# Early rows gathered once, from candidates of both column halves: an attention and expert-routing kernel with a speculative first group

## The chip, the core and the metric

The kernel runs on one core of one Trainium2 chip. The metric is device time in microseconds, the median of three runs. The engines are TensorE (PE; its weight loads are listed as PEld), VectorE (DVE), ScalarE (ACT), GpSimd (POOL) and SyncE (SP), which here does nothing but issue transfers. The 16 DMA engines serve SyncE's queue and GpSimd's gathers and scatters. TensorE's clock has two levels, 2.4 and 1.2 GHz; the profile shows which was granted as 1.00 and 0.50.

## What is computed

Block-local attention, then a mixture of experts with a capacity:

```python
# q, k, v: (8, 8, 576, 64); blocks of 64 positions
scores = scale * q_c @ k_c.T          # inside each block
attn = softmax(scores); out = attn @ v_c
x = out.transpose(0, 2, 1, 3).reshape(4608, 512)

logits = x @ w_gate                   # 8 experts
expert_idx = argmax(logits); gate_w = its softmax probability
for e in range(8):
    tok = tokens with expert_idx == e
    if len(tok) > capacity: keep the `capacity` (80) with the largest gate_w
    out[tok] = gate_w * (relu(x[tok] @ w1[e]) @ w2[e])   # w1: 512x1024, w2: 1024x512
# tokens that are not kept have zero rows
```

## The kernel before

**Attention, 0 to about 113 us.** 18 pairs of half tiles run through one pipeline written out by hand (`scores`, `maxima`, `minus`, `probs`, `values`, `divide`, `store`). The rows go to a scratch array `xs` in memory, and at the same time through a transposition (`xtrans`) and the gate product (`gate_mm`, `gate_copy`, `gate_sum`), four tiles of 128 tokens at a time. `values(35)`, `xtrans(17)`, `gate_mm(8)` are the last of these.

**Which tokens are kept.** A token's gate probability is turned into one of 256 levels. For each tile, `signs` (on ScalarE) or `steps_` (on VectorE) compare all levels with each token's, and `tally` sums these over the tokens of an expert by short matmuls; `left_add` adds them up in `left`. `threshold` counts the levels that at least `capacity` tokens reach. Tokens at or over the threshold become candidates: they are numbered by prefix sums, one-hot matrices (`hot`) move their row numbers and keys into a table (the matmuls of line 1034, into `two`), and exact ranks select 80 of them (lines 1042 to 1131). `place` then writes the row numbers of the expert slots, GpSimd gathers those rows, and `experts` runs the two layers in groups of 128 slots.

**The speculative first group.** From the first 28 tiles alone the kernel guesses a stricter threshold for experts 0 and 1 (`spec_count` to `spec_slot`) and numbers 64 early rows of each in `ptc`. `spec_hot` makes one-hots of that number on VectorE, in three groups of 10, 9 and 9 tiles (`SHOT`). `spec_cand` multiplies them with the tokens' row numbers (`comp`), and `spec_gather` sums three pieces into an index `gi0` and has GpSimd gather the rows into `x0`. `spec_units` cuts the first group's two expert layers into 19 units of work: 3 of transpositions and 16 of matmuls, each four column groups wide. `fill(k)` puts the next k units into TensorE's order, between the short steps of the selection. Each engine works strictly in program order. So where `fill(1)` puts the first unit, the transposition of `x0`, TensorE waits until the gather has landed.

`keep_warm(n)` puts n matmuls of 256 columns whose result nobody reads into TensorE's order.

**Transfers.** SyncE issues in program order: the last stores to `xs` and pieces of the weights of experts 0 and 1 (`early_pieces`), then the 2 MB loads of the other experts' weights (line 1155) with nine zeroings of the output (`clear`, 1 MB each) between them. Those loads go into buffers laid over memory of the attention stage, so each waits for the last use of what lay there; the first of them lies over `pk0`, which holds the early one-hots. The six scatters of result rows (line 266) wait until all zeroings have landed.

Of the kernel before, what the change touches and what calls it, by code (L numbers as in the profile page):

```python
# [8 lines left out]
F32 = mybir.dt.float32  # L9
BF16 = mybir.dt.bfloat16  # L10
# [7 lines left out]
P = 128  # L18
# [23 lines left out]
S0 = 64  # L42
# [16 lines left out]
def attention_moe(ctx: ExitStack, tc: tile.TileContext, qk, vv, wg, w1, w2, cap, cst, out):  # L59
# [116 lines left out]
    def rows(t, at, n=NT * 512):  # L176

        return nc.gpsimd.indirect_dma_start(
            out=t, out_offset=None, in_=xs[0:n, :],
            in_offset=bass.IndirectOffsetOnAxis(ap=at, axis=0),  # L180
            bounds_check=n - 1, oob_is_err=False)
# [117 lines left out]
    with ExitStack() as actx:  # L299
# [432 lines left out]

        def spec_hot(r0, n):
            if 'hot0' not in S:
                S['hot0'] = wk.tile([P, 3, S0, 10], BF16, name="pk0", tag="qb1", bufs=1), deque(range(3))
            oh = S['hot0'][0][:, S['hot0'][1].popleft()]
            nc.vector.tensor_tensor(
                oh[:, :, 0:n], S['io_h'][:, 0:S0, 0:n],
                S['ptc'][:, None, r0:r0 + n].to_broadcast([P, S0, n]), op=ALU.is_equal)
            S['oh0', r0] = oh  # L740

        def spec_cand(r0, n):
            oh = S['oh0', r0]
            if 'cand0' not in S:
                S['cand0'] = ps1.tile([P, 2, 512], F32, name="xw0", tag="tp")[:, 0]
            cand0 = S['cand0'][0:S0, 0:12].rearrange("p (k e) -> p k e", e=2)
            k = 2 * S.setdefault('chunk0', 0)
            S['chunk0'] += 1
            for j in range(n):
                rt = r0 + j  # L750
                nc.tensor.matmul(
                    cand0[:, k:k + 2, :],
                    lhsT=oh[:, :, j], rhs=comp[:, rt, 0:2, 0:2], start=j == 0, stop=j == n - 1)

        def spec_gather():
            gi0 = mp.tile([P, 2], I32, name="gi0")
            with nc.allow_low_precision(reason="row numbers are whole and far below 2^24"):
                nc.vector.tensor_reduce(
                    gi0[0:S0], S['cand0'][0:S0, 0:12].rearrange("p (k e) -> p e k", e=2),
                    axis=AX.X, op=ALU.add)  # L760
            x0 = S['x0'] = mp.tile([P, DM], F32, name="x0")
            for e in range(2):
                rows(x0[S0 * e:S0 * e + S0], gi0[0:S0, e:e + 1], 6 * 576)

        units = deque()

# [68 lines left out]
        with tc.manual_schedule():  # L835
# [117 lines left out]
            spec_pos()  # L953
            values(35, "s")
            spec_slot()
            for r0, n in SHOT:
                spec_hot(r0, n)
            xtrans(16)
            gate_mm(7)
            gate_copy(7)  # L960
            for j in range(24, 28):
                signs(j)
            for r0, n in SHOT:
                spec_cand(r0, n)
            divide(34)
            spec_gather()
            divide(35)
            store(17)
            early_pieces(20)
            gate_sum(7, gates)  # L970
            pops(2)
            spec_own()
            xtrans(17, ("o", "s"))
            gate_mm(8)
            flush(gates)
            gate_copy(8)
# [4 lines left out]
            two = ps1.tile([P, 2, 512], F32, name="two", tag="s")  # L981
            S['warm'] = [ps1.tile([P, 512], F32, name=("xw", "hw", "pwarm")[j], tag=f"o{j}") for j in range(3)]
            spec_units()
            signs(28)
            signs(29)
            gate_sum(8, gates)
            tally(24, 4)
            fill(1)
            pops(2)
            signs(30)  # L990
            signs(31)
            left_add(24)
            flush(gates)
            rest(32, "sum")
            signs(32)
            for j in range(33, 36):
                steps_(nc.vector, j)
            fill(1)
            tally(28, 4)
            left_add(28)  # L1000
            spec_keep()
            fill(1)
            tally(32, 4)
            fill(1)
            threshold()
            rest(32, "inverse", "key")
            fill(1)
            mask = gk.tile([P, NE, RT], BF16, name="mask", tag="mask", bufs=1)
# [313 lines left out]
```

## Time and profile before

| | |
|---|---|
| median of 3 runs | 240.28 us (239.45 to 240.59) |
| the profiled execution | 242.49 us, span of its trace 240.6 us |
| TensorE busy | 220.5 us, 92% of the span |
| VectorE, ScalarE, GpSimd busy | 118.5, 69.4, 54.3 us |
| moved by DMA | 84.73 MB, 352 GB/s over the span |
| mean granted TensorE clock | 0.958 |

The busy times are sums over stages with different limits, and a matmul at half clock counts as busy for longer. What the change is worth is to be read from the stage between the end of attention and the first expert row, about 112 to 154 us, and from what the end of the kernel waits for.

### The profile page before, as it was taken

To read this page: it belongs to the slowest core of one execution; us is meant where nothing else is said; L and a number is where in the kernel's file an instruction comes from. 1 tells how busy PE (TensorE), PEld (TensorE's weight loads), DVE (VectorE), ACT (ScalarE), POOL (GpSimd) and SP (SyncE) were. 2 spreads that over 40 slices of the span, in tenths; PEclk is the share of its full clock that TensorE was granted. 3 is DMA by queue.
4 is the path that set the end of the run, shared out by engine and by line. 5 is a ranking of instruction groups with operands and counts; after the bars stand their busy time and mean duration, and the time that the engine had idled before them with its cause. 6 is when DMAs were issued, how large, how long until landed. Compare 5 with 4: busy or idle time off the path is not lost.

```text
span 240.6 us, 7297 instructions
## 1 busy us (share of the span) xinstructions
PE 220.5 (92%) x3161; PEld 139.0 (58%) x3161; DVE 118.5 (49%) x270; ACT 69.4 (29%) x123; POOL 54.3 (23%) x155
## 2 busy tenths in 40 slices
PE   8789998999999999999866989899999999999960
PEld 5689887888888898987743253234334333333310
DVE  7857686777877778788432457401111112111110
ACT  2214333453645455455423151111002011010000
POOL 9300402022322222236230351420000000000631
PEclk9999999999999999999855799999999999999997
DMA  6999999999999999999999969999999999998221
GB/s 254 403 408 378 333 396 408 410 409 405 402 395 393 379 407 332 356 352 408 395 293 399 396 240 308 412 332 362 369 406 408 403 388 399 397 408 312 99 94 40
DMA packets 34758, 84.73 MB, mean 352 GB/s; under 512 B 3038, under 2 KB 3166, under 8 KB 34720
## 3 DMA queue, kind: packets, MB, share of 16 engines
q1 hardware_dynamic: 33744, 81.31, 90.0%
q0 software_dynamic: 976, 2.88, 3.3%
q8 instruction: 27, 0.44, 0.7%
q14 instruction: 11, 0.09, 0.1%
HBM read 64.00 MB, written 20.45 MB: 351 GB/s over the span
## 4 chain that ended last, share of the span: by engine, by line
PE 78%; DMA 10%; issue 3%; ACT 2%; SPq 2%; DVE 2%; POOL 1%; POOLq 0%
PE hc L214 13%; PE o L437 12%; PE s L380 12%; PE yc L247 11%; PE px L409 4%; PE pt L409 4%; DMA qb<-in_qk 4%; DMA w<-in_w 3%; DMA x<-xs,gi 3%; PE hw L794 3%; PE yfirst L247 3%; PE small L489 3%; PE hw L785 2%; PE hpc L232 2%; PE hfirst L214 2%
## 5 line engine op out<-in xcount | busy, mean ns | idle before, releaser
L437 PE MATMUL o<-vb,pT 128*64 128x130 f32 x576 | 36.1, 276 | 0.6 <-ACT pT L418 0.5
L380 PE MATMUL s<-qb 128*64 128x128 f32 x512 | 31.9, 276 | 2.7 <-DMA qb<-in_qk 1.8
L437 PEld LDWEIGHTS o<-vb,pT 128*64 128x64 f32 x576 | 31.6, 135 | 1.8 <-ACT pT L418 0.6
L214 PE MATMUL hc<-w,xtc 128*32 128x512 f32 x288 | 32.5, 594 | 0.0
L380 PEld LDWEIGHTS s<-qb 128*64 128x64 f32 x512 | 27.9, 137 | 5.1 <-issue 3.7
L391 DVE TENSOR_REDUCE mx<-s 128x16 f32<-128x1024 f32 x18 | 22.0, 1225 | 14.7 <-PE s L380 13.9
L247 PE MATMUL yc<-w,htc 128*32 128x512 f32 x256 | 28.2, 592 | 0.0
L418 ACT ACTIVATE pT<-pt 128x1024 f32<-128x1024 f32 x18 | 18.3, 1025 | 30.8 <-PE pt L409 29.2
L480 ACT COPY xT<-px 128x1024 f32<-128x1024 f32 x17 | 17.1, 1008 | 25.5 <-PE px L409 25.5
L452 DVE TENSOR_TENSOR x<-o,rc 128x1024 f32<-128x1024 f32 (+1 forms) x20 | 22.4, 1118 | 0.7
L396 DVE TENSOR_TENSOR sm<-s,mx 128x1024 f32<-128x1024 f32 x18 | 22.1, 1228 | 0.6
L214 PEld LDWEIGHTS hc<-w,xtc 128*32 128x32 f32 x288 | 8.8, 110 | 19.4 <-issue 19.4
L247 PEld LDWEIGHTS yc<-w,htc 128*32 128x32 f32 x256 | 8.2, 110 | 18.7 <-issue 18.7
L266 POOL DMA_INDIRECT out<-x,to x1 | 1.0, 1048 | 65.4 <-DVE htc L236 65.4
L219 ACT ACTIVATE hsc<-hc 128x512 f32<-128x512 f32 x4 | 2.4, 598 | 46.4 <-PE hc L214 46.4
L590 ACT ACTIVATE lv<-io_b,bo 128x256 bf16<-128x256 bf16 x33 | 14.2, 498 | 0.3 <-DVE bo L570 0.3
L221 DVE TENSOR_SCALAR hsc<-hc 128x512 f32<-128x512 f32 x5 | 3.5, 690 | 21.8 <-PE hc L214 21.8
L252 DVE TENSOR_SCALAR ysc<-yc,gatec 128x512 f32<-128x512 f32 x4 | 3.0, 751 | 21.2 <-PE yc L247 21.2
L409 PE MATMUL pt<-ct,sm 64*128 64x64 f32 x288 | 12.8, 229 | 0.0
L409 PE MATMUL px<-ct,x 64*128 64x64 f32 x272 | 12.4, 229 | 0.2 <-issue 0.2
L236 DVE COPY htc<-hpc 128x512 f32<-128x512 f32 x5 | 3.5, 692 | 18.3 <-PE hpc L232 18.3
L409 PEld LDWEIGHTS pt<-ct,sm 64*128 64x128 f32 x288 | 10.3, 139 | 2.9 <-issue 2.8
(211 smaller groups left out, 260.8 us busy)
## 6 DMA issues: line engine op xcount, KB each, us to landing
w<-in_w SPq DMA_DIRECT2D x12, 2048.0 KB, 15.0
qb<-in_qk SPq DMA_DIRECT2D x32, 512.0 KB, 8.1
vb<-in_vv SPq DMA_DIRECT2D x36, 260.0 KB, 7.1
out<-zero SPq DMA_DIRECT2D x9, 1024.0 KB, 16.0
xs<-x SPq DMA_DIRECT2D x16, 512.0 KB, 7.6
w<-in_w SPq DMA_DIRECT2D x16, 512.0 KB, 8.1
w<-in_qk SPq DMA_DIRECT2D x4, 512.0 KB, 4.9
xs<-x SPq DMA_DIRECT2D x4, 256.0 KB, 6.1
```

The lines of the kernel that those rows point to most:

```text
L214: nc.tensor.matmul(h[o:o + 32, :], lhsT=xT[r][:, b, o:o + 32], rhs=getw(groups[r][g])[0][:, b, 512 * f:512 * f + 512], start=(b == 0), sto ...
L247: nc.tensor.matmul(y[o:o + 32, :], lhsT=hT[r][c // 4][:, c % 4, o:o + 32], rhs=getw(groups[r][g])[1][:, c, :], start=(c == 0), stop=(c == ...
L380: nc.tensor.matmul(ps[64 * u:64 * u + 64, t, P * pr:P * pr + P].rearrange("p (h k) -> p h k", h=2), lhsT=t8[:, 1, pr, u, :], rhs=t8[:, 0:3 ...
L391: nc.vector.tensor_reduce(d['mx'], d['s8'], axis=AX.X, op=ALU.max)
L396: nc.vector.tensor_tensor(d['sm'].rearrange("p c k h -> p h c k"), d['s8'], d['mx'][:, :, :, None].to_broadcast([P, 2, 8, 64]), op=ALU.sub ...
L409: nc.tensor.transpose(at[:, 64 * c:64 * c + 64], src(c)[rows], ident[rows, rows])
L418: nc.scalar.activation(d['pT'], pt, AF.Exp, scale=0.125)
L437: nc.tensor.matmul(po[64 * u:64 * u + 64, o:o + 130].rearrange("p (h x) -> p h x", h=2), lhsT=d['pT'][:, u, c:c + 64], rhs=v[:, :, pr, u, ...
L452: nc.vector.tensor_tensor(TT[T][:, r:r + nt, :].rearrange("p r (k h e) -> p (r k) h e", k=4, h=2), pov[..., 0:64], rc[:, :, :, None].to_br ...
L480: nc.scalar.copy(XT[n].rearrange("p c u j -> p u c j"), pm.rearrange("p u (c j) -> p u c j", j=64))
L489: nc.tensor.matmul(pl[32 * j:32 * j + 32].rearrange("p (u j) -> p u j", u=2), lhsT=wgp[:, pr], rhs=XT[2 * T + j // 2][:, 4 * (j % 2) + pr] ...
L590: nc.scalar.activation(lv, io_b, AF.Sign, bias=bo[:, rt:rt + 1], scale=-1.0)
```

## The change

It alters the speculative group and the order around it in these ways:

- The candidate matmuls write a table of 128 rows, expert 0 into the lower 64 and expert 1 into the upper 64 (`tile_position` picks the half of the array's columns); each tile takes two matmuls with 2 columns in place of one with 4. Behind each group stands one filler matmul.
- One gather of 128 rows takes the place of two of 64.
- The third group's nine one-hots are made on GpSimd (`spec_hot1`).
- A copy of one column into a spare part of `pk0` follows the gather on GpSimd. The first large weight load lies over `pk0`, so it now waits for this copy.
- Two groups of candidates stand ahead of the last transposition and one behind it; the index sum stands behind it too.
- Up to the threshold one unit is left, after the sums of tiles 28 to 31, and 15 fillers stand where there were 2. `threshold` stands ahead of the next unit, and the levels of tile 32 are made on VectorE.

```diff
         def spec_hot(r0, n):
             if 'hot0' not in S:
-                S['hot0'] = wk.tile([P, 3, S0, 10], BF16, name="pk0", tag="qb1", bufs=1), deque(range(3))
+                S['hot0'] = wk.tile([P, 4, S0, 10], BF16, name="pk0", tag="qb1", bufs=1), deque(range(3))
...
+        def spec_hot1(r0, n):
+            oh = S['oh0', r0] = S['hot0'][0][:, S['hot0'][1].popleft()]
+            pf = gk.tile([P, SPEC], F32, name="ptf", tag="ptf", bufs=1)
+            nc.gpsimd.tensor_copy(pf[:, r0:r0 + n], S['ptc'][:, r0:r0 + n])
+            for j in range(n):
+                nc.gpsimd.tensor_scalar(oh[:, :, j], ct[:, C_IO + P:C_IO + P + S0],
+                                        pf[:, r0 + j:r0 + j + 1], None, op0=ALU.is_equal)
+
         def spec_cand(r0, n):
...
-                nc.tensor.matmul(
-                    cand0[:, k:k + 2, :],
-                    lhsT=oh[:, :, j], rhs=comp[:, rt, 0:2, 0:2], start=j == 0, stop=j == n - 1)
+                for e in range(2):
+                    nc.tensor.matmul(
+                        cand0[S0 * e:S0 * e + S0, k:k + 2], lhsT=oh[:, :, j], rhs=comp[:, rt, 0:2, e],
+                        start=j == 0, stop=j == n - 1, tile_position=(0, S0 * e))
+                if j == n - 1:
+                    nc.tensor.matmul(S['cand0'][:, 1, 0:2 * P], lhsT=ones_b, rhs=io_b,
+                                     start=True, stop=True)
 
         def spec_gather():
...
-            for e in range(2):
-                rows(x0[S0 * e:S0 * e + S0], gi0[0:S0, e:e + 1], 6 * 576)
+            rows(x0, gi0, 6 * 576)
+            nc.gpsimd.tensor_copy(S['hot0'][0][:, 3, 0, 0:1], S['ptc'][:, 0:1])
...
             spec_slot()
-            for r0, n in SHOT:
-                spec_hot(r0, n)
+            spec_hot(*SHOT[0])
+            spec_hot(*SHOT[1])
+            spec_hot1(*SHOT[2])
             xtrans(16)
...
-            for r0, n in SHOT:
-                spec_cand(r0, n)
             divide(34)
-            spec_gather()
+            spec_cand(*SHOT[0])
             divide(35)
+            spec_cand(*SHOT[1])
             store(17)
...
             xtrans(17, ("o", "s"))
+            spec_cand(*SHOT[2])
+            spec_gather()
             gate_mm(8)
...
-            signs(28)
-            signs(29)
             gate_sum(8, gates)
             tally(24, 4)
-            fill(1)
+            keep_warm(5)
             pops(2)
-            signs(30)
-            signs(31)
+            for j in range(28, 32):
+                signs(j)
             left_add(24)
...
-            signs(32)
-            for j in range(33, 36):
+            for j in range(32, 36):
                 steps_(nc.vector, j)
-            fill(1)
+            keep_warm(5)
             tally(28, 4)
             left_add(28)
             spec_keep()
             fill(1)
+            keep_warm(3)
             tally(32, 4)
+            threshold()
             fill(1)
-            threshold()
```

What this does to VectorE's order, from the early one-hots (`pk`) to the next tiles' gate sums; `x` with `rc` is the division of tiles 34 and 35, `gi` the index sum. Before:

```order
L737 TENSOR_TENSOR pk_2222<-io_h,ptc 128x64x9 x2
L450 TENSOR_SCALAR rc_2300<-o_2175 128x8
L451 RECIPROCAL rc_2300<-rc_2300 128x8
L452 TENSOR_TENSOR x_2131<-o_2175,rc_2300 128x512
L758 TENSOR_REDUCE gi_2304<-xw_2271 64x2
L450 TENSOR_SCALAR rc_2313<-o_2209 128x8
L451 RECIPROCAL rc_2313<-rc_2313 128x8
L452 TENSOR_TENSOR x_2131<-o_2209,rc_2313 128x512
L559 TENSOR_REDUCE gm_2324<-small 128x4
```

And with the change:

```order
L452 TENSOR_TENSOR x_2131<-o_2175,rc_2281 128x512
L450 TENSOR_SCALAR rc_2307<-o_2209 128x8
L451 RECIPROCAL rc_2307<-rc_2307 128x8
L452 TENSOR_TENSOR x_2131<-o_2209,rc_2307 128x512
L559 TENSOR_REDUCE gm_2337<-small 128x4
L526 TENSOR_TENSOR sh_2333<-small,gm_2337 128x32
L724 TENSOR_REDUCE cnt<-mine 128x8
L476 COPY xT_2367<-px17s 128x512
L770 TENSOR_REDUCE gi_2389<-xw_2285 128x1
```

The index sum stood between the two divisions and now stands behind both and behind the copy of the last transposition.

GpSimd at the same place, from its last work for the keys to the levels of tiles 28 to 31 (`u`, `lb`). Before:

```order
L552 CAST comp<-r_1995 128x4x8
L178 DMA x_2306<-xs,gi_2304 64x512 x2
L564 TENSOR_SCALAR u_2327<-sx_2326 128x4
L567 TENSOR_SCALAR lb_2328<-u_2327 128x4
L556 TENSOR_SCALAR bb_2330<-lb_2328 128x4
```

And with the change:

```order
L552 CAST comp<-r_1995 128x4x8
L745 CAST ptf<-ptc 128x9
L747 TENSOR_SCALAR pk_2222<-ct,ptf 128x64 x9
L178 DMA x_2391<-xs,gi_2389 128x512
L773 COPY pk_2222<-ptc 128x1
L564 TENSOR_SCALAR u_2340<-sx_2339 128x4
```

A cast, nine one-hots and the one-column copy are new there, and one gather is gone.

TensorE, from the sums of tiles 24 to 27 (the last of them uses `lv_2269`, with the change `lv_2279`) to the count for the threshold (line 630); lines 778 and 785 are units (788 and 795 with the change), 663 fillers, and `lv_2431` (`lv_2470`) belongs to tile 31. Before:

```order
L612 MATMUL small_2389<-mine,lv_2269 128x8
L778 MATMUL xw<-ct,x_2306 128x128 x4
L785 MATMUL hw<-w_0_103,xT_2394 32x512 x2
L785 MATMUL hw<-w_1_1957,xT_2394 32x512 x2
...
L663 MATMUL pwarm<-io_b,ones_b 128x256
...
L612 MATMUL small_2389<-mine,lv_2431 128x8
L785 MATMUL hw<-w_0_103,xT_2394 32x512 x2
...
L630 MATMUL small_2389<-ge,ones_b 128x8
```

And with the change:

```order
L612 MATMUL small_2428<-mine,lv_2279 128x8
...
L663 MATMUL pwarm<-io_b,ones_b 128x256
...
L607 MATMUL small_2428<-mine,ones_b 128x8
...
L612 MATMUL small_2428<-mine,lv_2470 128x8
L788 MATMUL xw<-ct,x_2391 128x128 x4
...
L612 MATMUL small_2428<-mine,lv_2488 128x8
...
L630 MATMUL small_2428<-ge,ones_b 128x8
L795 MATMUL hw<-w_0_103,xT_2433 32x512 x2
```

The transposition of `x0`, for which TensorE waits, moved behind the sums of tiles 28 to 31, and three units of four matmuls moved behind the count.

## Rows read from the trace of the kernel before

**Rows 1.** Chain of waits, 112 to 160 us: start, length, what
```profile
118.13 0.16 DVE gi L758
120.12 7.29 DMA x<-xs,gi
127.55 1.10 PE xw L778 x4
134.06 0.12 PE small L607
134.42 1.42 PE hw L785 x8
136.01 0.17 DVE thr L633
154.40 0.86 PE xpc L203 x4
```

**Rows 2.** Windows: busy times by engine; granted clock, DMA share, GB/s stand last
```profile
114.80:118.00 3.20, 3.20 (x28) 3.20 (x28) 0.06 (x1) 1.74 (x5) 0.00 (x0) 1.00 1.04 402
118.20:135.20 17.00, 12.10 (x112) 6.44 (x115) 6.29 (x30) 3.90 (x10) 3.81 (x9) 0.50 1.02 356
```

**Rows 3.** Timeline of VectorE, 124 to 131 us
```profile
124.42 0.19 DVE L559 TENSOR_REDUCE gm<-small 128x4 f32<-128x32 f32 x1 [2.65 <-PE small L612]
129.42 0.19 DVE L563 TENSOR_REDUCE sx<-ex 128x4 f32<-128x32 f32 x1 [4.14 <-ACT ex L527]
130.46 0.68 DVE L595 TENSOR_SCALAR lv<-io_b,bo 128x256 bf16<-128x256 bf16 x3
```

**Rows 4.** Timeline of TensorE: candidates, and a unit's matmuls at either clock
```profile
114.79 3.30 PE L751 MATMUL xw<-comp,pk 128*64 128x4 bf16 x28 [0.18 <-ACT xT L480]
132.12 1.94 PE L785 MATMUL hw<-w,xT 128*32 128x512 f32 x8
145.54 1.06 PE L785 MATMUL pwarm<-w,xT 128*32 128x512 f32 x8
```

**Rows 5.** Timeline of GpSimd, its last stretch: the stores of the tokens
```profile
223.69 1.05 POOL L266 DMA_INDIRECT out<-x,to  x1 [65.39 <-DVE htc L236]
229.59 0.98 POOL L266 DMA_INDIRECT out<-ysc,to  x1 [0.28 <-issue]
234.22 0.98 POOL L266 DMA_INDIRECT out<-ysc,to  x1 [3.45 <-DVE ysc L252]
```

**Rows 6.** Windows, 140 to 220 us: clock, DMA share and GB/s stand last
```profile
140.00:160.00 20.00, 18.18 (x197) 7.68 (x195) 9.11 (x51) 4.07 (x11) 7.33 (x10) 1.00 0.88 305
160.00:220.00 60.00, 60.00 (x550) 20.72 (x552) 8.47 (x12) 7.20 (x13) 0.00 (x0) 1.00 1.04 395
```

**Rows 7.** Timeline of TensorE: rows from which prices are taken
```profile
107.17 2.00 PE L437 MATMUL o<-vb,pT 128*64 128x130 f32 x32 [0.45 <-ACT pT L418]
112.88 0.71 PE L409 MATMUL px<-ct,x 64*128 64x64 f32 x16
10.08 0.72 PE L857 MATMUL small<-warm 128*128 128x256 bf16 x5
```

**Rows 8.** Timeline of GpSimd: rows from which prices are taken
```profile
118.59 1.22 POOL L178 DMA_INDIRECT x<-xs,gi  x1 [5.55 <-DVE rc L451]
140.86 1.21 POOL L656 TENSOR_SCALAR pk<-ct,ptok 128x128 bf16<-128x128 f32 x2
148.04 1.12 POOL L178 DMA_INDIRECT xgc<-xs,gic  x1 [5.98 <-DVE bt L1056]
```

**Rows 9.** Timeline of SyncE's issues: the first large weight loads
```profile
120.33 8.57 SPq L1155 DMA_DIRECT2D w<-in_w  x3
```

**Rows 10.** Line L178, the row gathers: issue to landing
```profile
DMA to landing us min/median/max: 8.2/8.9/8.9
```

**Rows 11.** DMA queues from 122 to 123 us
```profile
q1 hardware_dynamic: 116, 0.21, 81.8%
q0 software_dynamic: 25, 0.06, 16.4%
```

More of the change, by code (lines that the diff above doesn't have):

```diff
@@ L744, in spec_cand @@
             if 'cand0' not in S:
-                S['cand0'] = ps1.tile([P, 2, 512], F32, name="xw0", tag="tp")[:, 0]
-            cand0 = S['cand0'][0:S0, 0:12].rearrange("p (k e) -> p k e", e=2)
+                S['cand0'] = ps1.tile([P, 2, 512], F32, name="xw0", tag="tp")
+            cand0 = S['cand0'][:, 0]
             k = 2 * S.setdefault('chunk0', 0)
@@ L750, in spec_cand @@
                 rt = r0 + j
-                nc.tensor.matmul(
-                    cand0[:, k:k + 2, :],
-                    lhsT=oh[:, :, j], rhs=comp[:, rt, 0:2, 0:2], start=j == 0, stop=j == n - 1)
+                for e in range(2):
[5 more added lines that the diff above has]
+                                     start=True, stop=True)
         def spec_gather():
-            gi0 = mp.tile([P, 2], I32, name="gi0")
+            gi0 = mp.tile([P, 1], I32, name="gi0")
             with nc.allow_low_precision(reason="row numbers are whole and far below 2^24"):
-                nc.vector.tensor_reduce(
-                    gi0[0:S0], S['cand0'][0:S0, 0:12].rearrange("p (k e) -> p e k", e=2),
-                    axis=AX.X, op=ALU.add)
+                nc.vector.tensor_reduce(gi0, S['cand0'][:, 0, 0:6], axis=AX.X, op=ALU.add)
             x0 = S['x0'] = mp.tile([P, DM], F32, name="x0")
-            for e in range(2):
-                rows(x0[S0 * e:S0 * e + S0], gi0[0:S0, e:e + 1], 6 * 576)
+            rows(x0, gi0, 6 * 576)
+            nc.gpsimd.tensor_copy(S['hot0'][0][:, 3, 0, 0:1], S['ptc'][:, 0:1])
         units = deque()
```

## The prediction

> **What bounds the kernel now.** I read the chain of waits first, then the engines' timelines at the places it names, then the clock, then the end.
>
> The chain has one long piece that is no engine's work: the second gather of the early rows is issued at 120.12 and lands 7.29 us later, and TensorE's four transpositions of those rows (line 778) start at 127.55 [rows 1]. TensorE is in order, so all that stands behind them waits too: the sums over the last tiles, the threshold at 136.01, and through that everything up to the first transposition of an expert row at 154.40. From there TensorE works to the end without a gap worth naming.
>
> The clock is the second thing to see. Over the 28 candidate matmuls (114.8 to 118.0) it is granted in full, right after them it falls to half, and it stays there for 17.0 us [rows 2]. Ahead of the fall TensorE did nothing but matmuls of 4 columns; the four early units behind the gather then ran at half clock.
>
> Third, a side chain: VectorE starts the last tile's gate sums at 124.42, but its next exponential sits on ScalarE behind the copy of those same transposed rows, so the sum comes at 129.42 and the levels' steps only at 130.46 [rows 3]. So the gather holds two chains at once.
>
> At the far end the six stores of tokens are not free to move. The first starts at 223.69, when the zeroing of the output has landed; they follow each other (the fifth at 229.59, so 1.475 us each); only the sixth, at 234.22, waits for TensorE's last product [rows 5]. The DMA engines are full from 160 to 220 us (share 1.04) and have room only before: 0.88 over 140 to 160, that is 2.4 us [rows 6]. A gain of TensorE beyond some 3 us therefore meets this second chain.
>
> **The change, part by part.**
>
> *Candidates.* 28 matmuls become 56, each for one half of the output columns. The old ones go at 3.30/28 = 118 ns [rows 4]. The trace has no pair of 64-wide halves with two columns; the nearest is line 437, which alternates between the same two column halves with far longer rows and takes 2.00 us for 32, 60 ns each [rows 7]. I take 60 (118 is the other bound): 38 ahead of the last transposition, 2.3 us, and 18 behind it, 1.1. Each of the three groups gets one filler of 256 columns, 0.11 us by the five that take 0.72 with their latency [rows 7].
>
> *Their place.* In the order the divisions of tiles 34 and 35 no longer stand around the index sum on VectorE, so the last transposition has its input early. TensorE: 114.79, plus 2.3 and two fillers, plus 0.9 for one gate transposition and 16 half transpositions (0.71 for 16 [rows 7]), plus 1.1 and a filler: 119.4. The index is summed by 119.6, where it was 118.13 [rows 1], so this part alone loses 1.3 us.
>
> *Nine one-hots on GpSimd.* Two 128x128 compares take 1.21 there, 0.61 each [rows 8]; one of 128x64 costs between half of that, 0.31, and all of it. Since a part of it is fixed I take 0.43. From about 113.6 (input, older work and a short cast done) nine end at 117.5, bounds 116.4 and 119.1. TensorE wants the first at 118.2 and the ninth at 119.3, so they are hidden, but at the upper bound with nothing to spare. Without that cover each tenth of a microsecond more in one costs 0.9 in the gather. VectorE is relieved of a third of its one-hots, which hides behind the wait for TensorE.
>
> *One gather for two.* GpSimd took 1.22 for the first and started the second 1.53 after it [rows 1, 8]. The one gather starts at 119.9 and leaves GpSimd at 121.1. Behind it stands a copy of one column, then the last tiles' levels: these start about when they did.
>
> *Loads held.* The first large weight load was issued at 120.33 [rows 9]; now it waits for that small copy, 121.6: 1.3 us later, and behind it on SyncE wait all the other loads and the zeroing. But the last store of rows and the last weight piece are issued some 3 us earlier, since the division that they wait for no longer stands behind the index sum, so the DMA engines still have them to move until about 123, and a load issued at 121.6 moves its first bytes about then. I count 0.5 us lost, between 0 and 1.3.
>
> *When the rows land.* 7.29 us from issue before, for the second half [rows 1]; 8.2 to 8.9 for most gathers of 128 rows among full queues [rows 10]; one issued at 148.04 [rows 8] was there for the transposition at 154.40, so under 6.4. With no large load queued ahead of it I take 6.5: 126.4.
>
> *Rule and row.* From 122 to 123 us the gathers' queue had 16.4% of the DMA engines' time and the loads' queue 81.8% [rows 11]: what stands in the loads' queue does slow a gather. The Trainium skill says otherwise: in "DMA: Bandwidth & Descriptors", section "Queues, rings and completion order", a DMA engine takes turns between its queues packet by packet, so a gather would have its turns whether or not loads are queued, and holding them would buy nothing. That is the second rival below.
>
> *The order behind it.* Ahead of the transpositions now stand fillers in place of units, and the sums of tiles 28 to 31; the last sums and the threshold follow directly, without the three units that stood between. The exponential is no longer behind the rows' copy: with the gate transposition about 3.3 us earlier, the steps are done near 124 (131.1 before), the ScalarE signs near 124.5, and the sums of tiles 28 to 31 near 125. So the gather is still the last to arrive, but by 1.4 us. From 126.4: transposition 0.55 (half of the 1.10 at half clock [rows 1]), three fillers 0.33, the last sums, comparison and count 0.5 (from 134.0 to 136.01 less the unit of 1.42 that stood between [rows 1]): threshold at 127.8, which is 8.2 earlier.
>
> *Units given back.* Three units that ran before the threshold now run after it. One is about 0.99 us at full clock (8 records in 1.06 with latency [rows 4]). One of the three hides: between the threshold and the main candidates TensorE waits for GpSimd, whose two one-hots end at 140.86 + 1.21 = 142.07 [rows 8], 6.1 after the threshold. Two lie bare: 2.0. So the expert stage starts 6.2 earlier, at 148.2. TensorE shows no wait for a weight (busy 60.00 of 60.00 from 160 to 220 [rows 6]), and the later loads are issued as TensorE frees their buffers, so they move with it.
>
> **The sum.** By TensorE the sixth store could start at 234.22 - 6.2 = 228.0. By the other chain: the zeroing lands 2.4 earlier (the room of 140 to 160 is filled, since the buffers that those loads wait for come free 6 to 8 us sooner) less 0.5, so the first store starts at 221.8, and the sixth five steps later, 229.2. The later of the two counts: 5.0 us gained. The profiled execution took 242.49 for a span of 240.6, and would take 237.5; it is 2.2 over the median of the runs, 240.28, from which I forecast **235.3**. Its own bounds: 234.0 (nothing lost by holding, all room used) to 236.7 (a landing at 128).
>
> **The rivals.**
>
> *Holding buys nothing* (the rule above): the gather lands 8.9 after 119.9, at 128.8; TensorE gains 3.8 and is now the later chain: 236.5. For it: other gathers of 128 rows took that long. Against it: the shares of rows 11.
>
> *The clock is lost all the same.* The early matmuls are as narrow as before, with one filler to a group, and TensorE is nearly idle from 121 to 126. Then transposition and fillers cost 0.9 more, and about six microseconds of units run at half clock (in the old run the units begin about 129.3, behind the 1.10 of transpositions and their copy, and the clock is back at 135.2; a unit's records take 1.94 at half clock against 1.06 [rows 4]), which loses 3.0: TensorE gains 2.3, 238.0. Against it: 38 narrow matmuls take less time than the 28 did, and transpositions and fillers stand among them.
>
> *The index comes late*: 118 ns for each of the 56, or GpSimd's one-hots at their upper bound. The index is 3.3 later, the loads too, the DMA engines run dry for about 3 us ahead of the first load, and the zeroing is no earlier than before. About 239.2; with the lost clock as well, no change: the change would not do what it says.
>
> *Slower.* The units taken out ahead of the threshold are what brought the clock back. If fillers don't, it stays at half well into the units after the threshold. At half clock each microsecond there costs half of one; the 5.3 us left of TensorE's gain after its 0.9 are used up if it is not back by about 139 (127.8 + 0.9 + 10.6). If it takes until 143, TensorE is 1.8 behind and the run takes 242.1.
>
> **How the numbers follow.** Forecast 0.42; holding buys nothing 0.14; lost clock 0.20; late index 0.10; both together, no change, 0.04; slower 0.10. A change within 0.5% (1.2 us) can hardly be told from none with runs that spread from 239.45 to 240.59. Faster by more than that: the first three and a third of the late ones, 0.79. Same: the rest of the late ones and the 0.04, 0.11. Slower 0.10. The range leaves out the slow case and half of those near no change: 233.6 to 239.4.
>
> **What would show it.** Right: the granted clock is 1.00 from 114 to 140; candidate matmuls at some 60 ns; the index sum near 119.6; the rows' transposition near 126.4 with the tile sums 28 to 31 ahead of it; the threshold near 128; the first expert transposition near 148; the first store near 222 and no wait of the sixth on VectorE. Wrong, if half clock shows after 118, if GpSimd's one-hots pass 119, if the first store still starts at 223 or later, or if TensorE waits for weights after 150.

## The result, and the profile after

The changed kernel takes 237.37 us (median of 18 runs, 235.11 to 240.12); the kernel before, beside it on the same chip, takes 240.78 us (18 runs, 239.18 to 242.55). The ratio is 0.9845, 95% interval 0.9818 to 0.9872: faster by 1.55%, or 3.7 us. A second comparison, in the experiments, gave 236.84 against 241.34. The ratios leave out runs more than 1.5% above the fastest of the same kernel and the medians keep them, so the two can differ. The forecast was 235.3, its range 233.6 to 239.4.

The profiled execution took 237.37 us for a span of 235.5; before, 242.49 and 240.6. So the two traces differ by 5.1, the medians by 3.4: the execution profiled before was 1.7 over the median that its kernel has in 18 runs. Of the 5.1, 4.2 are found below, from the first expert matmuls to the last store; 0.9 lies behind the last store's start (6.4 before, 5.5 after).

TensorE from the gate product to the first expert matmuls (start, length, engine, line, operation, tile; in brackets the idle time before it and what ended it):

```profile
120.41 2.79 PE L489 MATMUL small<-xT,wgp 128*32 128x128 f32 x32
...
126.28 0.18 PE L612 MATMUL small<-mine,lv 128*128 128x8 bf16 x1 [0.22 <-ACT lv L590]
126.68 0.18 PE L612 MATMUL small<-mine,lv 128*128 128x8 bf16 x1 [0.22 <-ACT lv L590]
...
126.92 0.64 PE L788 MATMUL xw<-ct,x 128*128 128x128 f32 x4
...
128.45 1.92 PE L795 MATMUL hw<-w,xT 128*32 128x512 f32 x16
130.78 1.92 PE L795 MATMUL hw<-w,xT 128*32 128x512 f32 x16
...
149.64 0.65 PE L203 MATMUL xpc<-ct,xgc 128*128 128x128 f32 x4
151.69 3.64 PE L214 MATMUL hfirst<-w,xtc 128*32 128x512 f32 x32 [1.39 <-issue]
```

The 7.29 us wait for the early rows [rows 1] is gone: their transposition (line 788) starts with no wait in front of it. What TensorE waits for now, just ahead of it, is ScalarE (`lv`, the signs of tiles 28 to 31). The first units behind the threshold (line 795, 16 records in 1.92) run at full clock.

The granted clock over that stage (busy times by engine; clock, DMA share and GB/s last):

```profile
114.80:117.80 3.00, 2.86 (x41) 2.59 (x41) 0.76 (x2) 1.87 (x5) 2.87 (x7) 0.97 1.06 404
117.80:124.50 6.70, 6.33 (x81) 4.97 (x81) 2.39 (x10) 1.08 (x3) 2.91 (x8) 0.50 1.02 372
124.50:140.00 15.50, 13.67 (x148) 7.61 (x145) 9.66 (x41) 6.00 (x18) 4.83 (x11) 1.00 1.02 396
```

It still falls behind the first two groups of candidates, but for 6.7 us in place of 17.0 [rows 2]. The gate product lies in those 6.7 us and takes 2.79.

VectorE (index sum, gate sums, levels, threshold) and ScalarE (exponential, signs, and the start of the selection):

```profile
120.52 0.16 DVE L770 TENSOR_REDUCE gi<-xw 128x1 int32<-128x6 f32 x1 [0.72 <-PE xw L764]
124.34 0.19 DVE L559 TENSOR_REDUCE gm<-small 128x4 f32<-128x32 f32 x1 [3.12 <-PE small L612]
126.15 0.87 DVE L595 TENSOR_SCALAR lv<-io_b,bo 128x256 bf16<-128x256 bf16 x4
128.56 0.17 DVE L633 TENSOR_SCALAR thr<-small 128x8 bf16<-128x8 f32 x1
130.89 0.46 DVE L1034 TENSOR_REDUCE ptok_b<-two 128x36 bf16<-128x288 f32 x1 [0.88 <-PE two L1028]
```

```profile
124.80 0.23 ACT L527 ACTIVATE ex<-sh 128x32 f32<-128x32 f32 x1 [1.29 <-DVE sh L526]
124.93 1.69 ACT L590 ACTIVATE lv<-io_b,bo 128x256 bf16<-128x256 bf16 x4
127.59 0.58 ACT L789 COPY xT<-xw 128x512 f32<-128x512 f32 x1 [0.97 <-PE xw L788]
132.77 0.60 ACT L799 ACTIVATE hs<-hw 128x512 f32<-128x512 f32 x1 [4.59 <-PE hw L795]
133.26 0.21 ACT L1036 CAST ptok<-ptok_b 128x36 f32<-128x36 bf16 x1
```

VectorE no longer waits 4.14 us for the exponential, which stood behind the rows' copy [rows 3]; the levels of the last tiles start at 126.15 (130.46 before) and the threshold stands at 128.56 (136.01). The last two rows show something new: the Relu of the first group (`hs`) waits 4.59 us for TensorE, and the cast `ptok`, whose input was ready at 130.89 + 0.46 = 131.35, stands behind it until 133.26. GpSimd's two one-hots of the selection wait for that cast (bracket of the third row here), and its stores come last:

```profile
113.68 3.98 POOL L747 TENSOR_SCALAR pk<-ct,ptf 128x64 bf16<-128x64 f32 x9
120.98 1.29 POOL L178 DMA_INDIRECT x<-xs,gi  x1 [3.31 <-DVE wt L530]
133.58 1.29 POOL L656 TENSOR_SCALAR pk<-ct,ptok 128x128 bf16<-128x128 f32 x2 [1.06 <-ACT ptok L1036]
219.47 1.05 POOL L266 DMA_INDIRECT out<-x,to  x1 [67.56 <-DVE htc L236]
229.99 0.98 POOL L266 DMA_INDIRECT out<-ysc,to  x1 [3.46 <-DVE ysc L252]
```

First and last store are both 4.2 us earlier than in [rows 5], and the last one still waits for TensorE's product, by as much as before. SyncE's issues, the first large loads and then the last five zeroings (195.62 before):

```profile
122.51 13.16 SPq L1165 DMA_DIRECT2D w<-in_w  x4
...
191.19 16.65 SPq L826 DMA_DIRECT2D out<-zero  x5
```

### The profile page after: what moved, and what is told of

Read it like the earlier page. It is cut to its first block, busy times and chain, and to the rows that moved or that the text cites. A ratio compares the mean times of both kernels' runs of the same rounds, so it can differ in the third digit from the quotient of the medians.

```text
span 235.5 us, 7389 instructions
## 1 busy us (share of the span) xinstructions
PE 219.6 (93%) x3203; PEld 140.2 (60%) x3203; DVE 118.0 (50%) x270; ACT 69.0 (29%) x122; POOL 57.0 (24%) x165
## 4 chain that ended last, share of the span: by engine, by line
PE 81%; DMA 7%; issue 3%; DVE 2%; SPq 2%; ACT 2%; POOL 0%; POOLq 0%
PE hc L214 13%; PE o L437 12%; PE s L380 12%; PE yc L247 11%; PE pt L409 4%; PE px L409 4%; PE small L489 4%; DMA qb<-in_qk 4%; DMA w<-in_w 3%; PE hw L804 3%; PE yfirst L247 3%; PE hpc L232 2%; PE pwarm L795 2%; PE hw L795 2%; PE hfirst L214 2%
## 5 line engine op out<-in xcount | busy, mean ns | idle before, releaser
L391 DVE TENSOR_REDUCE mx<-s 128x16 f32<-128x1024 f32 x18 | 22.0, 1221 | 14.7 <-PE s L380 13.6
L247 PEld LDWEIGHTS yc<-w,htc 128*32 128x32 f32 x256 | 8.2, 110 | 18.7 <-issue 18.7
L252 DVE TENSOR_SCALAR ysc<-yc,gatec 128x512 f32<-128x512 f32 x4 | 3.0, 752 | 21.2 <-PE yc L247 21.2
L590 ACT ACTIVATE lv<-io_b,bo 128x256 bf16<-128x256 bf16 x32 | 13.6, 498 | 0.0
```

The source lines that it names most:

```text
L247: nc.tensor.matmul(y[o:o + 32, :], lhsT=hT[r][c // 4][:, c % 4, o:o + 32], rhs=getw(groups[r][g])[1][:, c, :], start=(c == 0), stop=(c == ...
L391: nc.vector.tensor_reduce(d['mx'], d['s8'], axis=AX.X, op=ALU.max)
L590: nc.scalar.activation(lv, io_b, AF.Sign, bias=bo[:, rt:rt + 1], scale=-1.0)
```

## The experiments

Twelve kernels, in three sets of four; those of one set ran on one chip, beside the kernel before.

**Parts of the change (before in this set: 242.09 us).** First the hold alone was taken away, then one half of the change at a time was done, then all sixteen new fillers were taken out.

*No hold.* The changed kernel without the one-column copy.

```diff
             rows(x0, gi0, 6 * 576)
-            nc.gpsimd.tensor_copy(S['hot0'][0][:, 3, 0, 0:1], S['ptc'][:, 0:1])
```

> The changed kernel without the one-column copy on GpSimd, so the first large load waits only for the last candidate matmul (about 120.2 instead of 122.5). If holding the loads is what brings the rows in early: rows land 1.5 to 2.5 us later (near 127 instead of 125.3), TensorE waits for them ahead of the last sums, threshold near 130 instead of 128.6, and about 238.5. If queues take turns anyway, as the second rival has it: rows land within 0.5 us of 125.3, threshold unchanged, 237.4 or a little less, since the loads start 2.3 us earlier.

239.77 us, ratio 0.980 (0.9722 to 0.9878); its runs lie between 235.8 and 242.5, so the time settles nothing. In the trace the first load is issued at 119.97, and TensorE waits 2.11 us for the rows, until 128.91. The same edit is tried again below, on a kernel whose runs lie closer together.

*Only the new order behind the gather*, put into the kernel before (two gathers, old candidates).

```diff
             tally(24, 4)
-            fill(1)
+            keep_warm(5)
...
+            threshold()
             fill(1)
-            threshold()
```

> The kernel before with only the order behind the gather changed (signs, fillers, units and threshold as in the changed kernel); candidates, two gathers and early loads as before. If the order carries the gain: the exponential no longer waits behind the rows' copy, rows land at 127.4 as before, threshold near 129.7, clock back by 126 thanks to the fillers, and about 238 (gain 2.5 to 3). If the early landing carries it: threshold near 133, about 240.

239.53 us, ratio 0.9832 (0.9758 to 0.9905). In its trace the rows come as late as before, and the threshold stands all the same at 128.95:

```profile
127.32 0.63 PE L778 MATMUL xw<-ct,x 128*128 128x128 f32 x4 [0.69 <-DMA x<-xs,gi]
```

```profile
128.95 0.17 DVE L633 TENSOR_SCALAR thr<-small 128x8 bf16<-128x8 f32 x1
```

*Only the new gather*, with its candidates, one-hots and hold, and the old order behind it.

```diff
             tally(24, 4)
-            keep_warm(5)
+            fill(1)
...
-            threshold()
             fill(1)
+            threshold()
```

> The changed kernel with the old order behind the gather: two signs first, units between the sums, threshold behind the third, no fillers but the two old ones and the three of the candidates. Rows land near 125.3. If the order carries the gain: exponential still behind the rows' copy, the units at half clock, threshold 7 to 8.6 us after the landing, so 133 to 134, about 239 to 239.5 (gain 1.5 to 2). If the landing carries it: about 237.5.

238.44 us, ratio 0.9878 (0.9821 to 0.9935). By the ratios the new order alone is worth 4.1 us and the new gather alone 3.0, while the whole change has 3.7 above and 4.5 in its second comparison, each with some 1 to 2 us either way. So the whole is not the sum of its halves, and nothing here shows that it gives more than the order alone.

The traces show the overlap. The attention stage ahead of the candidates ends at another time in each execution (the first candidate matmul starts at 113.16 here, at 114.79 before), so the threshold is counted from that matmul: 21.2 us before, 18.7 with the gather alone, 14.2 with the order alone, 13.6 with both. With the gather alone TensorE waits 2.02 us for the rows, until 124.42, VectorE waits 3.01 us for the exponential, which stands behind their copy as it did in [rows 3], and the threshold comes at 131.90:

```profile
124.42 1.12 PE L788 MATMUL xw<-ct,x 128*128 128x128 f32 x4 [2.02 <-DMA x<-xs,gi]
```

```profile
126.32 0.19 DVE L563 TENSOR_REDUCE sx<-ex 128x4 f32<-128x32 f32 x1 [3.01 <-ACT ex L527]
131.90 0.17 DVE L633 TENSOR_SCALAR thr<-small 128x8 bf16<-128x8 f32 x1 [0.75 <-PE small L630]
```

*No fillers.*

```diff
-                if j == n - 1:
-                    nc.tensor.matmul(S['cand0'][:, 1, 0:2 * P], lhsT=ones_b, rhs=io_b,
-                                     start=True, stop=True)
...
-            keep_warm(5)
...
-            keep_warm(5)
...
-            keep_warm(3)
```

> The changed kernel without its 13 new fillers and the 3 of the candidates. If the fillers bring the clock back: half clock from 118 to 131 or later instead of 124.5, the four units ahead of the main candidates take 1.9 instead of 1, threshold about as before (128.5), first expert transposition 2 to 3 us later, about 239.5 to 240. If the clock comes back by the units alone: within 0.5 of 237.4.

238.74 us, ratio 0.9884 (0.983 to 0.9939), where the changed kernel has 0.9845 and 0.9814: 0.9 to 1.7 us slower, by intervals that overlap. In the trace the price is paid behind the threshold, where the first 16 records of line 795 (here 792) take 3.64 in place of 1.92. TensorE of this kernel, and its clock ahead of that place and over it:

```profile
127.46 3.64 PE L792 MATMUL hw<-w,xT 128*32 128x512 f32 x16
```

```profile
118.20:121.40 3.20, 3.20 (x46) 2.73 (x44) 1.20 (x6) 0.26 (x1) 1.75 (x4) 0.50 1.04 397
121.60:124.80 3.20, 1.61 (x22) 0.96 (x20) 1.97 (x13) 1.99 (x6) 1.21 (x5) 1.00 1.05 389
125.00:131.50 6.50, 5.91 (x42) 2.44 (x42) 2.61 (x10) 0.58 (x1) 2.71 (x8) 0.50 1.03 402
```

Here the clock came back at about 121.5 without a new filler, and fell a second time near 125. So that the fillers bring it back is not shown; what this execution has, and the two of the changed kernel have not, is the second fall ahead of the threshold. Nor do fillers rule out a fall behind it: in the trace of the new order alone, which has 13 of them, the clock was at half from about 129.3 to 132.7.

**What binds now (before in this set: 241.34 us).** The trace after named two orders on ScalarE and the half clock ahead of the gate product. Each got a kernel, with the changed kernel once more beside them.

> The changed kernel once more, so that the three variants beside it can be compared on one chip. Its ratio to the kernel before should again be near 0.984, that is 3.5 to 4.5 us faster. Its profiled execution should again show half clock from about 118 to 124 us, the gate product behind the candidates at 2.8 us, and the sums of tiles 28 to 31 (not the early rows) as the last thing ahead of the threshold.

236.84 us (236.21 to 239.08), ratio 0.9814 (0.9759 to 0.9869). Its profiled execution, 239.08, shows the same stage, and a second fall of the clock:

```profile
126.00:134.00 8.00, 6.75 (x74) 3.29 (x74) 5.91 (x16) 2.38 (x7) 4.03 (x10) 1.00 1.02 396
135.50:142.00 6.50, 6.48 (x38) 2.64 (x37) 2.01 (x12) 0.68 (x4) 0.00 (x0) 0.51 1.02 398
```

That is behind the stretch in which TensorE waits for the late cast. In the execution shown above the same wait (0.77 and 0.30 us in both) had no such sequel.

*The Relu later.* `S['relu']()` is called behind ScalarE's one-hots.

```diff
-                if b == 3:
+                if b == 3 and f == 0:
+                    S['relu'] = lambda: nc.scalar.activation(hs[:, 0:512], h, AF.Relu)
+                elif b == 3:
```

> The changed kernel with one step moved: the Relu of the first group's first four column blocks (one ScalarE instruction of 0.60 us, which waits for TensorE's unit until 132.8) goes behind the cast of the candidate numbers and ScalarE's four one-hots. Theory (the stall after the threshold is ScalarE's order): the cast starts at about 131.4 in place of 133.3, GpSimd's two one-hots end near 134.3, the main candidates end 1 to 1.9 us earlier, and the kernel is 0.8 to 1.7 us faster than the changed one. Rival (TensorE is bound there anyway by the units given back, and the wait for GpSimd is filled by units): the cast comes earlier but the first expert transposition moves by less than 0.3 us, and the time is the same.

234.91 us, ratio 0.9727 (0.967 to 0.9784): 1.9 us faster than the changed kernel beside it. ScalarE:

```profile
130.99 0.22 ACT L1038 CAST ptok<-ptok_b 128x36 f32<-128x36 bf16 x1 [3.20 <-DVE ptok_b L1036]
...
133.80 0.59 ACT L799 ACTIVATE hs<-hw 128x512 f32<-128x512 f32 x1
```

The cast now waits for its own input alone. The first expert transposition stands at 147.93, 19.8 us behind the threshold at 128.17 (21.1 in the changed kernel's first execution), and no second fall of the clock shows. The theory holds; the time gained is slightly more than its 1.7, of which this trace carries 1.3 against that execution.

*More fillers among the candidates.*

```diff
-                if j == n - 1:
+                for _ in range(0 if j < n - 1 else 4 if r0 < 19 else 1):
```

> The changed kernel with four filler matmuls in place of one behind each of the first two groups of candidates (six more of 0.11 us, 0.66 us in all). Theory (the narrow candidate matmuls are what the clock falls after): with wide matmuls among them the clock stays at its full level from 117.8 to 124.5 us, the gate product takes about 1.0 in place of 2.8 us, the signs and the threshold come 1 to 1.8 us earlier although the index sum is 0.4 to 0.7 later; net 0.5 to 1.2 us faster. Rival (six more fillers are not enough, or the clock falls for the short gate matmuls and the wait behind them): the half clock shows at the same place, and the kernel is 0.5 to 0.9 us slower.

237.48 us, ratio 0.9809 (0.9742 to 0.9877): no gain, and no loss that the ratios show, so the time settles neither theory nor rival. The clock did hold longer, to about 121.3, which is 5.7 us behind the first candidate matmul in place of 2.7, and then fell under the gate product itself, which took 2.65.

```profile
114.00:121.40 7.40, 7.21 (x133) 6.21 (x131) 3.73 (x13) 3.65 (x8) 4.19 (x10) 0.99 1.05 403
121.60:125.00 3.40, 3.03 (x43) 2.33 (x39) 0.42 (x4) 0.27 (x1) 2.90 (x8) 0.54 0.97 337
```

*Two signs ahead of the exponential.*

```diff
+            signs(28)
+            signs(29)
             gate_sum(8, gates)
...
-            for j in range(28, 32):
+            for j in range(30, 32):
```

> The changed kernel with the signs of tiles 28 and 29 (two ScalarE instructions of 0.42 us) ahead of the last tiles' gate sums and their exponential. Theory (the sums of tiles 28 to 31 wait for ScalarE, which does the exponential first): the last of the four signs ends 0.6 to 0.8 us earlier, near 125.9 in place of 126.6, the early rows' transposition starts near 126.2, and the kernel is 0.4 to 0.8 us faster. Rival (the levels of tiles 32 to 35, which need that exponential, then come 0.8 us later and decide the threshold instead): the threshold stays within 0.3 us and the time is the same.

235.22 us, ratio 0.9747 (0.9688 to 0.9807): 1.6 us faster than the changed kernel beside it, by intervals that overlap, where 0.4 to 0.8 was expected. From the start of the candidates to the threshold's sum the profiled executions take 13.0 us (115.21 to 128.24) against 13.6 (114.94 to 128.56) in the changed kernel, or 13.4 in its second profile. That carries 0.4 to 0.6. The rest is not explained by the edit; part of it may be the second fall of the clock, which this execution doesn't have and the profiled one of the changed kernel beside it has.

**Both orders, and parts of the change on top of them (before in this set: 241.54 us).**

> The changed kernel with both orders on ScalarE altered: the first Relu behind the cast of the candidate numbers and ScalarE's one-hots, and the signs of tiles 28 and 29 ahead of the last exponential. Theory (two separate stalls, one ahead of the threshold and one behind it): both hold, the threshold about 0.5 us after the time of the Relu alone less 0.6, the main candidates' GpSimd one-hots not behind a late cast; some 2 to 3 us faster than the changed kernel, that is a ratio to the kernel before of 0.968 to 0.974. Rival (both variants only moved where the clock falls, and one of them is enough): no faster than the variant with the late Relu alone, ratio 0.973 or more, and the profile shows a fall of the clock after 132 us.

Both edits above together: 234.43 us, ratio 0.9708 (0.9663 to 0.9753). This is the fastest median of the study, 7.1 us under the kernel before it ran beside, but the interval overlaps that of the late Relu alone (0.9727): that the second edit adds anything to the first is not shown. Nor do the traces show it: from the first candidate matmul to the last store it takes 113.3 us here and 112.5 with the late Relu alone.

*The same, without the hold.* The one-column copy is taken out as in the first experiment.

> As the kernel with both orders altered, but without the one-column copy on GpSimd that holds the large loads behind the gather. Theory (loads queued ahead of the gather's rows slow it): the first load is issued about 1 to 2.5 us earlier, the gather takes 7 to 9 us from its issue in place of 4.5 to 5.5, TensorE waits for the early rows 2 to 3 us, the clock is at half again when they come, and the kernel is 1.5 to 4 us slower than with the hold. Rival (the queues take turns, so the hold is worth nothing, and the loss seen without it before was the clock of those runs): the gather lands as early and the time is the same or better by the earlier loads.

236.55 us, ratio 0.9771 (0.9727 to 0.9814): slower than with the hold, by 2.1 us in the medians and 1.5 in the ratios. TensorE waits for the rows again, and the threshold comes 14.3 us behind the first candidate matmul in place of 13.2:

```profile
127.38 0.66 PE L787 MATMUL xw<-ct,x 128*128 128x128 f32 x4 [1.40 <-DMA x<-xs,gi]
```

The queues show what differs (packets, MB, share of the 16 engines' time; q0 carries the gather, q1 the loads). Without the hold, from 123 to 124 us, 2.5 to 3.5 behind the gather's start at 120.48, and from 125 to 126:

```profile
q1 hardware_dynamic: 132, 0.43, 106.5%
...
q1 hardware_dynamic: 55, 0.23, 55.1%
q0 software_dynamic: 47, 0.19, 47.4%
```

With the hold, from 121 to 122 us, 1.7 to 2.7 behind the gather's start at 119.32:

```profile
q0 software_dynamic: 25, 0.10, 42.9%
q1 hardware_dynamic: 86, 0.16, 41.4%
```

Without it not one packet of the gather moves in that microsecond, while the loads queued ahead fill the engines; with it the rows flow 2.7 us after the start at the latest. The first kernel without the hold shows the same: no packet of the gather from 123 to 125 us, 2.3 to 4.3 behind its start.

*The same, with the third group's one-hots on VectorE.*

```diff
-            spec_hot1(*SHOT[2])
+            spec_hot(*SHOT[2])
```

> As the kernel with both orders altered, but the nine one-hots of the third group are again one VectorE instruction (about 0.42 us longer on VectorE, between the other two groups and the division of tile 34) and GpSimd's ten instructions are gone. Theory (that part of the change hides work of 0.42 us of VectorE, which holds the division of tile 34 and with it the first candidates): candidates, index and all behind them 0.3 to 0.5 us later, the kernel 0.2 to 0.6 us slower. Rival (it is hidden, or GpSimd's one-hots cost VectorE time while both run): no difference, within 0.3 us either way.

234.56 us, ratio 0.9721 (0.9677 to 0.9766), against 234.43 and 0.9708: no difference. The rival holds; this part of the change buys nothing that can be measured.

*The same, with two levels on VectorE.*

```diff
             signs(28)
             signs(29)
+            steps_(nc.vector, 30)
+            steps_(nc.vector, 31)
             gate_sum(8, gates)
...
-            for j in range(30, 32):
-                signs(j)
```

> As the kernel with both orders altered, but the levels of tiles 30 and 31 are compared on VectorE (two of about 0.22 us) ahead of the last gate sums, where VectorE waits for TensorE, in place of two on ScalarE behind the exponential. Theory (the sums of tiles 28 to 31 still wait for ScalarE): these sums are done near 125, the early rows are again the last to arrive, the threshold comes 0.3 to 0.8 us earlier, and the kernel is 0.3 to 0.8 us faster. Rival (the rows land at about 126 and decide): the threshold stays within 0.2 us, the last gate sums on VectorE come 0.3 us later, and the time is the same.

234.88 us, ratio 0.9702 (0.9655 to 0.9749): the same time. The sums of tiles 28 to 31 are through near 125, and now the rows are the last to arrive:

```profile
126.30 0.66 PE L788 MATMUL xw<-ct,x 128*128 128x128 f32 x4 [1.28 <-DMA x<-xs,gi]
```

The gather started at 120.32, so with held loads it took 6.0 us to here. ScalarE's signs and the gather end within 1.3 us of each other, and speeding up one shows the other.

## Why the prediction was nearly right, point by point

Of the signs that the prediction named for being wrong, one came: half clock shows after 118. Of those for being right, the 60 ns, the rows' transposition and the threshold came near, while the clock, the index, the expert stage, the first store and the last store's wait on VectorE missed.

**The candidates, the one-hots, the index.** 20 candidate matmuls take 1.29 us, 18 take 1.18: 60 ns as priced with a few more for latency. Nine one-hots end at 117.66 (117.5 predicted), each 0.44 (0.43), and are hidden as said. The index sum ran at 120.52, not 119.6: the clock fell at 117.8, before the last transposition and the third group, and the attention stage itself ended 0.15 later in this execution. The first load went out at 122.51 for 121.6.

**The gather.** Predicted: it would leave GpSimd at 121.1 and land at 126.4. It left at 122.3 and was there before 126.92, when TensorE took it up without a wait. That step failed, in the prediction's words "the gather is still the last to arrive, but by 1.4 us". The reason isn't mainly the gather: its estimate of 6.5 us from issue stands near the 6.0 of the last experiment. In the second execution of the changed kernel, issued at 120.68, it took

```profile
DMA to landing us min/median/max: 5.5/5.5/5.5
```

and so landed near 126.2. That this is close to the 126.4 forecast is luck: the start came 0.8 later than forecast and the way was 1.0 shorter. The gate chain was late.

**The step that failed first: the clock.** A granted clock of 1.00 from 114 to 140 was assumed, and half clock from 117.8 to 124.5 came. The gate product, for which the sum had about a microsecond, took 2.79, so the gate sums (`gm`) stand at 124.34, as late as the 124.42 of [rows 3], and not 3.3 earlier. Behind them ScalarE does the exponential before the four signs of 1.69 us, and the sums of tiles 28 to 31 end near 127, not 125. The prediction had these signs done near 124.5. So the threshold came at 128.56 for 127.8: 7.45 earlier, not 8.2. That is a small loss for a wrong chain, since the two that were confused end close together.

**Units given back.** Two bare units, 2.0 us, was the term, counted to the first expert transposition. From the threshold to there it was 136.01 to 154.40 = 18.4 before and 128.56 to 149.64 = 21.1 after, so 2.7; to the first expert matmul (`hfirst`, 155.92 before) 19.9 and 23.1, so 3.2. The prediction priced TensorE's work and its cover, GpSimd's two one-hots "6.1 after the threshold". These end at 133.58 + 1.29 = 134.87, 6.3 after it, close to that; but ScalarE's four one-hots start behind the Relu too, and TensorE's candidates, which wait for them, end at 136.4, 7.9 after the threshold in place of 6.3. The prediction did not list what the units, moved behind the threshold, put into ScalarE's order. Moving the Relu alone gave 1.9 us in the time and 1.3 in this stretch. Another 0.5 is the first expert copy: `hfirst` starts 2.05 after its transposition began, 1.52 before; this shows in some executions and not in others, and why stays open.

**The end.** The zeroing was to land only 1.9 us earlier and the stores' own chain to set the end. It landed 4.2 earlier, and TensorE set the end, as before. The estimate took the free share of the DMA engines from 140 to 160 [rows 6] as all the room there was. The last five zeroings are issued at 191.19 for 195.62: SyncE has them in order behind a load that waits for a buffer of TensorE's, so they moved with TensorE. The engines also moved more in the same share: 393 GB/s against 365 over the 16 and 20 us ahead of 140, by this view of both kernels (after, then before):

```profile
124.00:140.00 16.00, 14.17 (x159) 8.01 (x156) 9.81 (x41) 6.00 (x18) 5.07 (x13) 0.99 1.02 393
```

```profile
120.00:140.00 20.00, 15.60 (x144) 6.96 (x141) 8.13 (x31) 5.85 (x16) 5.99 (x15) 0.62 1.02 365
```

**The sum.** The miss of 2.1 is 0.5 of base (240.28 in three runs, 240.78 in eighteen) and 1.6 of gain: 5.0 forecast, 3.4 by the medians. For the profiled execution 237.5 was forecast and 237.37 came, but out of other terms: TensorE 4.2 in place of 6.2, no second chain, and 0.9 behind the last store that wasn't forecast at all. And the execution profiled before was 1.7 over its kernel's median, the one after at it, so the traces differ by more than the kernels do. The prediction saw this distance (2.2 to the three runs) and carried it over to the changed kernel as if it were constant. That step failed too; in which stage the 1.7 lay isn't known. That 237.5 and 237.37 agree is luck. Two side sums of the prediction don't come out of their own terms either: a landing at 128 leaves TensorE 4.6 of its 6.2, which gives 235.7 and not 236.7, and an index 3.3 late leaves it 2.9 and the stores' chain 3.1, which gives 237.4 and not 239.2.

**The rivals.** "Holding buys nothing" (listed first, though the prediction calls it the second rival) falls: by the shares of the DMA queues and by 1.5 to 2.1 us of time. The Trainium skill's rule behind it ("DMA: Bandwidth & Descriptors", section "Queues, rings and completion order": an engine goes round its queues packet by packet) does not alone foretell the trace without the hold, in which the gather's queue got 0 packets from 123 to 124 us beside 132 of the loads'. Whether the gather's packets stood in their queue by then no run shows; so what falls is the conclusion drawn from the rule, and how the loads delay the gather stays open. "The clock is lost all the same" was half right: it was lost ahead of the gate product and back at 124.5, ahead of the threshold. "The index comes late" came to 0.9 us and cost nothing, since the gather wasn't last. "Slower" needed the clock to be low well after the threshold. Without fillers it was, until about 131.7, and that kernel was 0.9 to 1.7 us slower than the changed one and still faster than the kernel before.

**What stays open.** What brings the clock back at 124.5, and how much its second fall near 135 costs on average; whether the new gather adds to the new order in time; why two signs ahead of the exponential give 1.6 us when the threshold moved by 0.4 to 0.6; and whether the gate product can be had at full clock, since the one attempt only moved the fall.

## What to carry to other kernels

When a stall is removed, list for each in-order engine what now stands ahead of the next input, the moved work's small followers included: here a Relu of 0.6 us on ScalarE, which had to wait for TensorE, cost 1.9 us, about as much as the two units that were counted. In this kernel it paid 1.5 to 2.1 us to start the gather that others wait for before large loads are queued, and a one-column copy of 0.2 us that makes those loads wait for it was a cheap way to say so. And the distance of one profiled execution from the median of its kernel doesn't carry over to the next kernel.

## What the runs showed of the hardware

- The granted clock fell behind matmuls of 2 columns while TensorE was listed as busy throughout (2.86 of 3.00 us), and six more fillers of 256 columns put the fall off, from 2.7 to 5.7 us behind the first of those matmuls, and not away. With one filler to a group, other executions had it from 2.0 to 4.1 us behind that matmul. The fall with the six came among the 32 short matmuls of the gate product.
- Equal waits of TensorE near 134 us (0.77 and 0.30 us) were followed by 6.5 us at half clock in one execution and by none in another of the same kernel.
- The clock came back at 124.5 behind fillers in the changed kernel, and at 121.5 with none before it in the kernel without fillers.
- From 2.5 to 3.5 us after the gather's start its packets didn't move beside a queue full of loads issued 0.75 us before it (119.73 and 120.48); 1.7 to 2.7 us after its start they did when the loads came behind it.
